# Cosine attention into a two-layer network on one core: one DMA transposition for a batch's x, two for its q, and a later draw of the later batches

## The chip, the cores and the metric

The kernel runs on one core of one Trainium2 chip. The metric is the device time of one execution in microseconds (us). It is the median of several executions, and before the change it is 295.16 us (three executions, 295.12 to 295.33). Batches are counted from zero here: "batch 2" is the third one.

## The reference, cut to what matters

```python
# q, k, v: [B=8, H=8, S=576, D=64] float32;  w_in: [512, 2048];  w_out: [2048, 512]
theta = pi / 2 * arange(S) / S
phi(x) = concat([max(x, 0) * cos(theta), max(x, 0) * sin(theta)], axis=-1)     # 64 -> 128 features
kv  = einsum('bhsf,bhsd->bhfd', phi(k), v)
z   = phi(k).sum(over s)
num = einsum('bhsf,bhfd->bhsd', phi(q), kv)
den = einsum('bhsf,bhf->bhs', phi(q), z) + 1e-6
x   = (num / den), heads side by side       # [B * S = 4608 tokens, 512]
h   = x @ w_in
out = max(0.01 * h, h) @ w_out              # [4608, 512] float32
```

## The kernel before, in words

**Tiling.** The 576 positions of a batch are cut into 512 ("main", four tiles of 128, index `j`) and 64 ("tail"). The main parts of the eight batches are groups `g` = 0 to 7 of 512 tokens; the eight tails together are group 8. A group goes through these stages:

- `load_q`, `load_k`, `load_v`: 1 MB each from HBM (`load_main`, L81), and 64-row tails of k and v in two small transfers each (`load_kvtail`, L91). All are issued by SyncE (SP).
- `q_prep` (L324): VectorE (DVE) writes phi(q) for one `j`, two instructions, into `qp`. `k_tail` and `k_main` (L247, L240) do the same for k into `kpt` and `kpm`; `v_main` and `v_tail` (L252, L255) cast v to 16 bits, on ScalarE (ACT) for batches 3 to 7.
- `q_transpose_dma` (L332): SP issues one DMA transposition for each `j`, `qp` to `qpT`. For batches 0 and 1 TensorE (PE) does it instead (`q_transpose`, L349).
- `kv_all` (L282): 40 small matmuls into a bank pair of PSUM, copied by ACT to `kv`. The ones appended to v make z a further column.
- `num` (L358): 8 matmuls of 66 columns, then `divide` (L372) on DVE, three instructions, which write `xs`. The pool `ps_n` has one buffer, so the `num` of the next `j` waits for the `divide` of this one.
- `x_transpose_dma` (L344) for each `j`: `xs` to `xT` by DMA. Batches 0 and 1 use PE (`x_transpose_half`), and batch 2 has PE transpositions of its own in four steps (`x_transpose`, L425): four 128x128 transpositions and an ACT copy each.
- `ffn1` (L434): for each of 16 tiles `m` of the hidden width, four matmuls of 512 columns of `xT`; ACT applies the leaky ReLU to two `m` at a time from `ps_h` (two buffers) to `g`.
- `ffn2` (L453): `g` times w_out into `ps_o`, four matmuls for each of 16 units, DVE copies each finished tile (`ffn2_out`, `osb`), and SP sends it out.

**Order.** The order is written out by hand, and each engine runs its own instructions strictly in that order. Groups 0 and 1 are a straight list. From there on `units` is the list of TensorE's `ffn1` and `ffn2` units, each at a position: a group takes 16 positions and 32 units, so half a position is one unit of four matmuls. `weave` (L588) puts every other step before the first unit whose position is not smaller. The steps' positions are set by `load_steps`, `kv_steps`, `q_steps` and `out_steps` (L692 to L716). The units of group g begin at position 16 g. They start with the first `ahead` units of `ffn2` of g alone, then `ffn1` of g+1 and the rest of `ffn2` of g alternate, and what is left of `ffn1` of g+1 ends the row.

**Buffers.** `qpp` (4), `qpT` (6), `xs` (4) and `xT` (2) are rotating pools; `qpp` also lends buffers to the x of groups 0 and 1. Each DMA carries one of eight completion semaphores in turn, so in the built program a DMA is issued only when the eighth DMA before it has landed.

Of the kernel before, what the change touches and what calls it, by code (L numbers as in the profile page):

```python
# [9 lines left out]
dt = mybir.dt  # L10
# [3 lines left out]
P = 128  # L14
J = 4
# [3 lines left out]
def kernel(  # L19
# [37 lines left out]
    kvtail = pool("kvtail", 4)  # L57
    qtail = pool("qtail", 2)
    kppool = pool("kpp", 2)
    qppool = pool("qpp", 4)  # L60
    qptpool = pool("qpT", 6)
    xspool = pool("xs", 4)
    small = pool("small", 3)
    xtpool = pool("xT", 2)
    gpool = pool("g", 2)
# [257 lines left out]

    def q_prep(g, j, lo=0, hi=H, eng=DVE):  # L324
        src, c, _ = q_src(g, j)
        if lo == 0:
            st["qp", g, j] = qppool.tile([P, H, F], dt.float16, name="qp", tag="qp")
        qp = st["qp", g, j]
        phi_half(eng, qp[:, lo:hi, 0:D], src[:, lo:hi], cos_t[:, c : c + 1])
        phi_half(eng, qp[:, lo:hi, D:F], src[:, lo:hi], sin_t[:, c : c + 1])  # L330

    def q_transpose_dma(g, j):  # L332
        qpT = qptpool.tile([P, H, P], dt.float16, name="qpT")
        nc.sync.dma_start_transpose(
            out=qpT, in_=st["qp", g, j].rearrange("p h f -> p (h f)")
        )
        st["qpT", g, j] = qpT

    def xT_tile(g, j):
        if ("xT", g) not in st:  # L340
            st["xT", g] = xtpool.tile([P, NKC, MAIN], dt.float16, name="xT")
        return st["xT", g][:, :, j * P : (j + 1) * P]

    def x_transpose_dma(g, j):  # L344
        nc.sync.dma_start_transpose(
            out=xT_tile(g, j), in_=st["xs", g, j].rearrange("p h d -> p (h d)")
        )

    def q_transpose(g, j, eng, where="h"):  # L349
        qp = st["qp", g, j]  # L350
        ps = psum(where, [P, H, P], dt.float16, "ps_qt")
        for h in range(H):
            nc.tensor.transpose(ps[:, h, :], qp[:, h, :], ident)  # L353
        qpT = qptpool.tile([P, H, P], dt.float16, name="qpT")
        copy(eng, qpT, ps)
        st["qpT", g, j] = qpT

    def num(g, j, where="n"):  # L358
        qpT = st["qpT", g, j]
        ps = psum(where, [P, 2, 512], dt.float32, "ps_num")  # L360
        for h in range(H):
            for b, lo, hi in q_src(g, j)[2]:
                nc.tensor.matmul(  # L363
                    ps[lo:hi, h // 4, (h % 4) * NE : (h % 4 + 1) * NE],
                    lhsT=qpT[:, h, lo:hi],
                    rhs=kv[b][:, h, :],
                )
        xs = xspool.tile([P, H, D], dt.float16, name="xs")
        divide(ps, xs.rearrange("p (a b) e -> p a b e", a=2))
        st["xs", g, j] = xs  # L370

    def divide(ps, xs):  # L372
        den = small.tile([P, H], dt.float32, name="den")
# [15 lines left out]

    def num_half(g, jp, hg, where, ps=None):  # L390

        if hg == 0:
            st["xp", g, jp] = qppool.tile([P, 2, H, D], dt.float16, name="xp", tag="qp")
# [10 lines left out]
        divide(ps, st["xp", g, jp][:, :, 4 * hg : 4 * hg + 4, :])  # L404

    def x_transpose_half(g, jp, hg, ps=None):

        if ("xT", g) not in st:
            st["xT", g] = xtpool.tile([P, NKC, MAIN], dt.float16, name="xT")
        xp = st["xp", g, jp]  # L410
        out = ps is None
        if out:
            ps = psum("o", [P, 2, 2 * P], dt.float16, "ps_xth")
        for cc in range(2):
            for o in range(2):
                h = 4 * hg + 2 * cc
                nc.tensor.transpose(  # L417
                    ps[:, cc, o * P : (o + 1) * P], xp[:, o, h : h + 2, :], ident
                )
        if out:  # L420
            nc.scalar.copy(
                st["xT", g][:, 2 * hg : 2 * hg + 2, jp * 2 * P : (jp + 1) * 2 * P], ps
            )

    def x_transpose(g, j, where="o"):  # L425
        xs = st["xs", g, j]
        ps = psum(where, [P, NKC, P], dt.float16, "ps_xt")
        for c in range(NKC):
            nc.tensor.transpose(ps[:, c, :], xs[:, 2 * c : 2 * c + 2, :], ident)
        nc.scalar.copy(xT_tile(g, j), ps)  # L430

    def ffn1(g, m, lo=0, hi=MAIN, chunks=range(NKC), where="h"):  # L434

        if ("g", g) not in st:
            st["g", g] = gpool.tile([P, NFT, MAIN], dt.float16, name="g")
        if m % 2 == 0 and chunks[0] == 0 and lo == 0:
            st["h", m // 2] = psum(where, [P, 2, MAIN], dt.float32, "ps_h")
        xT = st["xT", g]  # L440
        ps = st["h", m // 2]
        for c in chunks:
            nc.tensor.matmul(  # L443
                ps[:, m % 2, lo:hi],
                lhsT=w1[m // 4, c][0][:, w1[m // 4, c][1], m % 4 : 512 : 4],
                rhs=xT[:, c, lo:hi],
                start=(c == 0 and lo == 0),
                stop=(c == NKC - 1 and hi == MAIN),
            )
        if m % 2 == 1 and chunks[-1] == NKC - 1 and hi == MAIN:  # L450
            nc.scalar.activation(st["g", g][:, m - 1 : m + 1, :], ps, AF.Lrelu)  # L451
# [202 lines left out]
    ps = psum("h", [P, 2, MAIN], dt.float16, "ps_x")  # L654
    for jp in range(2):
        x_transpose_half(1, jp, 0, ps[:, :, jp * 2 * P : (jp + 1) * 2 * P])
    nc.vector.tensor_copy(st["xT", 1][:, 0:2, :], ps)
    ffn2_out(0, 0, ACT)
    ffn2_mm(0, 1, 15, 16)
    ffn2_out(0, 1, ACT)  # L660
# [16 lines left out]
    for m in range(6, NFT):  # L677
        units.append((8 + m / 2, f1(1, m)))
    for g in range(1, NG):
        ahead = {1: 8, 2: 4}.get(g, 0)  # L680
        order = [f2(g, i) for i in range(ahead)]
        for i in range(16):
            if g + 1 < NG:
                order.append(f1(g + 1, i))
            if ahead + i < 16:
                order.append(f2(g, ahead + i))
        for n, u in enumerate(order):
            units.append((16 * g + 16 * n / len(order), u))
# [3 lines left out]
    def kv_steps(b, start, step, mm, eng_v, n_act=0):  # L692
        at(start - 0.01, kp_tiles, b)
        at(start, k_tail, b, DVE, DVE)
        for i in range(J):
            at(start + (i + 1) * step, k_main, b, i, ACT if i < n_act else DVE, DVE)
        v0, dv = (start + 1.5 * step, 1) if b > 3 else (start + 3 * step, 0.1)
        at(v0, v_main, b, 0, 4, eng_v)
        at(v0 + dv, v_main, b, 4, 8, eng_v)
        at(v0 + 2 * dv, v_tail, b, eng_v)  # L700
        at(mm, kv_all, b)
# [6 lines left out]
    def out_steps(b, start, step, lag):  # L708
        for j in range(J):
            at(start + j * step, num, b, j)  # L710
            at(start + j * step + lag, x_transpose_dma, b, j)

    def q_steps(b, start, step, lag):
        for j in range(J):
            at(start + j * step, q_prep, b, j)
            at(start + j * step + lag, q_transpose_dma, b, j)  # L716

    q_steps(2, 8, 0.4, 0.3)
    kv_steps(2, 9.7, 0.5, 14, DVE, 2)
# [56 lines left out]
```

## Time and profile before

| What | Value |
|---|---|
| median of three executions | 295.16 us |
| the profiled execution, its own time | 295.4 us |
| its span (first to last instruction) | 293.6 us |
| TensorE busy | 286.6 us, 98% |
| VectorE, ScalarE, GpSimd busy | 128.7, 118.3, 12.6 us |
| granted TensorE clock | 0.999 of full speed |
| DMA packets | 88,933, of which 56,912 under 512 B |
| HBM read and written | 36.70 and 9.44 MB |

The profiled execution is one execution, 0.24 us above the median. About 1.8 us of its time lie outside the span. Matmuls overlap in TensorE's pipeline, so the mean duration of one in the table of groups (373 to 379 ns for 512 columns) is longer than the distance from one start to the next: 0.86 us for four, 216 ns each, in the chain of waits.

### The profile page before, as it was taken

How to read it: one execution, taken by the hardware profiler on the slowest of the kernel's cores; microseconds unless marked ns; L12 is line 12 of the kernel's file. 1: busy time of each engine (PE TensorE's matmuls, PEld its weight loads, DVE VectorE, ACT ScalarE, POOL GpSimd, SP SyncE). 2: the span in 40 equal slices, each digit the busy share in tenths (PEclk: the TensorE clock that was granted, in tenths of full speed). 3: DMA queues.
4: the chain of work that ended last, by engine and by line, in shares of the span. 5: the costliest groups of instructions: out<-in, count | busy, mean ns of one | idle time of the engine just before them, and what ended most of it. 6: DMA issues, size and time to landing. Idle time of an engine off the chain costs nothing.

```text
span 293.6 us, 4865 instructions
## 1 busy us (share of the span) xinstructions
PE 286.6 (98%) x1958; PEld 152.6 (52%) x1958; DVE 128.7 (44%) x328; ACT 118.3 (40%) x148; POOL 12.6 (4%) x24
## 2 busy tenths in 40 slices
PE   8899999999999998999999999999999999999995
PEld 3585466555555554555545554555444444444444
DVE  6841687936836714923562346233333311000011
ACT  6856266753544631642453226322222232222200
POOL 2264000000000000000000000000000000000000
PEclk9999999999999999999999999999999999999999
DMA  7999999999999999989664998716671211011133
GB/s 230 346 387 407 321 362 335 313 193 334 200 285 320 180 258 343 163 173 332 170 148 84 279 259 180 111 54 143 136 169 56 71 54 38 36 45 59 42 70 73
DMA packets 88933, 56.93 MB, mean 194 GB/s; under 512 B 56912, under 2 KB 81744, under 8 KB 88528
## 3 DMA queue, kind: packets, MB, share of 16 engines
q1 hardware_dynamic: 88832, 56.57, 74.3%
q8 instruction: 15, 0.25, 0.4%
q10 hardware_dynamic: 80, 0.07, 0.1%
q14 instruction: 6, 0.05, 0.0%
HBM read 36.70 MB, written 9.44 MB: 157 GB/s over the span
## 4 chain that ended last, share of the span: by engine, by line
PE 88%; DMA 6%; SPq 3%; DVE 1%; ACT 1%; issue 0%; DVEq 0%
PE ps_h L443 40%; PE ps_o L466 39%; DMA ktl<-in_k_dram 3%; PE ps_num L363 2%; PE ps_kv L299 2%; DMA vst<-in_v_dram 2%; SPq L96 1%; SPq L86 1%; DMA out_dram<-osb 1%; PE ps_xth L417 1%; PE ps_qt L353 1%; PE ps_numh L399 1%; PE ps_kv L290 0%; PE ps_idle L166 0%; PE ps_kvh L274 0%
## 5 line engine op out<-in xcount | busy, mean ns | idle before, releaser
L443 PE MATMUL ps_h<-xT,w 128*128 128x512 f16 (+1 forms) x592 | 142.8, 373 | 0.1
L466 PE MATMUL ps_o<-w,g 128*128 128x512 f16 x560 | 139.5, 379 | 0.0
L451 ACT ACTIVATE g<-ps_h 128x1024 f16<-128x1024 f32 x72 | 73.2, 1023 | 125.2 <-PE ps_h L443 125.2
L443 PEld LDWEIGHTS <-w 128*128 128x128 f16 x592 | 64.4, 114 | 52.3 <-issue 0.2
L466 PEld LDWEIGHTS <-g 128*128 128x128 f16 x560 | 54.2, 98 | 61.4
L234 DVE COPY osb<-ps_o 128x512 f32<-128x512 f32 x31 | 21.4, 691 | 79.3 <-PE ps_o L466 78.5
L374 DVE TENSOR_SCALAR den<-ps_num 128x8 f32<-128x8 f32 x28 | 4.6, 165 | 51.0 <-PE ps_num L363 51.0
L379 DVE TENSOR_TENSOR xs<-ps_num,rden 128x512 f16<-128x512 f32 x28 | 19.4, 691 | 1.0
L226 DVE TENSOR_SCALAR kpm<-kst,sin_t 128x512 f16<-128x512 f32 (+1 forms) x40 | 16.6, 430 | 1.3 <-DMA kst<-in_k_dram 1.3
L226 DVE TENSOR_SCALAR qp<-qst,cos_t 128x512 f16<-128x512 f32 (+1 forms) x34 | 15.5, 456 | 2.7 <-DMA qst<-in_q_dram 2.7
L226 DVE TENSOR_SCALAR qp<-qst,sin_t 128x512 f16<-128x512 f32 (+1 forms) x34 | 15.5, 456 | 0.0
L232 ACT CAST vmain<-vst 128x1024 f16<-128x1024 f32 (+1 forms) x14 | 12.8, 919 | 6.0 <-DMA vst<-in_v_dram 5.9
L363 PEld LDWEIGHTS <-qpT 128*128 128x128 f16 (+1 forms) x256 | 10.6, 101 | 8.4 <-issue 3.1
L226 DVE TENSOR_SCALAR kpm<-kst,cos_t 128x512 f16<-128x512 f32 (+1 forms) x29 | 13.2, 454 | 0.4 <-DMA kst<-in_k_dram 0.3
L363 PE MATMUL ps_num<-kv,qpT 128*128 128x66 f16 (+1 forms) x256 | 11.8, 194 | 0.9 <-DVE xs L379 0.9
L166 PE MATMUL ps_idle<-blank 128*128 128x512 f16 x30 | 10.0, 483 | 1.2 <-DVE blank L161 1.2
L234 DVE CAST w<-w2st 128x1024 f16<-128x1024 f32 (+1 forms) x6 | 5.1, 868 | 11.5 <-DMA w2st<-in_moe_w_out_dram 11.4
L232 ACT COPY qpT<-ps_qt 128x1024 f16<-128x1024 f16 x7 | 7.0, 1012 | 6.0 <-PE ps_qt L353 6.0
L234 POOL CAST w<-w1st 128x1024 f16<-128x1024 f32 (+1 forms) x9 | 8.5, 946 | 3.4 <-DMA w1st<-in_moe_w_in_dram 3.3
L378 DVE RECIPROCAL rden<-den 128x8 f32<-128x8 f32 x36 | 7.3, 203 | 1.2
L299 PE MATMUL ps_kv<-vmain,kpm 128*128 128x66 f16 x192 | 7.2, 194 | 0.0
L306 ACT CAST kv<-ps_kv 128x528 f16<-128x528 f32 x6 | 3.6, 599 | 7.5 <-PE ps_kv L299 7.5
(62 smaller groups left out, 102.6 us busy)
## 6 DMA issues: line engine op xcount, KB each, us to landing
out_dram<-osb SPq DMA_DIRECT2D x32, 256.0 KB, 2.9
qst<-in_q_dram SPq DMA_DIRECT2D x7, 1024.0 KB, 6.9
kst<-in_k_dram SPq DMA_DIRECT2D x6, 1024.0 KB, 9.8
vst<-in_v_dram SPq DMA_DIRECT2D x6, 1024.0 KB, 9.0
w1st<-in_moe_w_in_dram SPq DMA_DIRECT2D x7, 512.0 KB, 10.3
w2st<-in_moe_w_out_dram SPq DMA_DIRECT2D x3, 1024.0 KB, 12.9
kst<-in_k_dram SPq DMA_DIRECT2D x4, 512.0 KB, 7.2
vst<-in_v_dram SPq DMA_DIRECT2D x4, 512.0 KB, 8.1
```

The source lines that it names most:

```text
L166: nc.tensor.matmul(ps, lhsT=blank[:, 0:P], rhs=blank)
L226: eng.tensor_scalar(out=o, in0=i, scalar1=0.0, scalar2=col, op0=ALU.max, op1=ALU.mult)
L232: nc.scalar.copy(o, i)
L234: eng.tensor_copy(o, i)
L299: nc.tensor.matmul(ps[:, h % 2, h // 2], lhsT=kpm[:, h, j, :], rhs=vmain[b % 2][:, h, j, :], start=False, stop=(h >= H - 2 and j == J - 1),)
L363: nc.tensor.matmul(ps[lo:hi, h // 4, (h % 4) * NE : (h % 4 + 1) * NE], lhsT=qpT[:, h, lo:hi], rhs=kv[b][:, h, :],)
L374: nc.vector.tensor_scalar_add(den.rearrange("p (a b) -> p a b", a=2), ps[:, :, D : 4 * NE : NE], 1e-6)
L378: nc.vector.reciprocal(rden, den)
L379: nc.vector.tensor_tensor(out=xs, in0=ps[:, :, 0 : 4 * NE].rearrange("p a (b e) -> p a b e", e=NE)[:, :, :, 0:D], in1=rden.rearrange("p (a ...
L443: nc.tensor.matmul(ps[:, m % 2, lo:hi], lhsT=w1[m // 4, c][0][:, w1[m // 4, c][1], m % 4 : 512 : 4], rhs=xT[:, c, lo:hi], start=(c == 0 an ...
L451: nc.scalar.activation(st["g", g][:, m - 1 : m + 1, :], ps, AF.Lrelu)
L466: nc.tensor.matmul(st["ps_o", g, tt], lhsT=st["g", g][:, m, tt * P : (tt + 1) * P], rhs=w2[:, m, :], start=(m == 0), stop=(m == NFT - 1),)
```

## The change

- q: two `j` share one `qp` tile and one `qpT` tile; `q_transpose_dma` transposes a pair (sixteen 128x128 blocks), two DMAs for a batch instead of four.
- x: `xs` is one tile for the whole batch, and `x_transpose_dma` transposes it in one DMA (sixteen blocks) after the last `divide`, instead of four of four blocks. `xT` is laid out as [128, j, chunk, 128], so the moving operand of `ffn1` is four pieces of 128 columns instead of 512 in a row. The pools become `qpp` 2, `qpT` 3, `xs` 1 of the larger tiles.
- Batch 2's x goes by DMA too; `x_transpose` is gone.
- Order: `ahead` is 14 and 8 instead of 8 and 4 for g = 1 and 2. Batch 3's k and v are loaded at 17.95 and 18 instead of 11 and 13, right behind batch 2's x transposition (17.9). The steps of batches 3 and 4 move later by 1 to 5 positions, the loads of batch 5 by 2, and the k and v steps of batches 5 to 7 by 1.5 at a step of 1.2 instead of 1.4.

```diff
-    qppool = pool("qpp", 4)
-    qptpool = pool("qpT", 6)
-    xspool = pool("xs", 4)
+    qppool = pool("qpp", 2)
+    qptpool = pool("qpT", 3)
+    xspool = pool("xs", 1)
...
-    def q_transpose_dma(g, j):
-        qpT = qptpool.tile([P, H, P], dt.float16, name="qpT")
+    def q_transpose_dma(g, jp):
         nc.sync.dma_start_transpose(
-            out=qpT, in_=st["qp", g, j].rearrange("p h f -> p (h f)")
+            out=qpT_pair(g, jp).rearrange("p o h t -> p (o h) t"),
+            in_=st["qp2", g, jp].rearrange("p o h f -> p (o h f)"),
         )
...
-            st["xT", g] = xtpool.tile([P, NKC, MAIN], dt.float16, name="xT")
-        return st["xT", g][:, :, j * P : (j + 1) * P]
+            st["xT", g] = xtpool.tile([P, J, NKC, P], dt.float16, name="xT")
+        return st["xT", g]
...
-    def x_transpose_dma(g, j):
+    def x_transpose_dma(g):
         nc.sync.dma_start_transpose(
-            out=xT_tile(g, j), in_=st["xs", g, j].rearrange("p h d -> p (h d)")
+            out=xT_tile(g).rearrange("p j c t -> p (j c) t"),
+            in_=st["xs", g].rearrange("p j h d -> p (j h d)"),
         )
...
-                rhs=xT[:, c, lo:hi],
+                rhs=xT[:, lo // P : hi // P, c, :],
...
-    nc.vector.tensor_copy(st["xT", 1][:, 0:2, :], ps)
+    nc.vector.tensor_copy(
+        st["xT", 1][:, :, 0:2, :], ps.rearrange("p c (j t) -> p j c t", j=J)
+    )
...
-        ahead = {1: 8, 2: 4}.get(g, 0)
+        ahead = {1: 14, 2: 8}.get(g, 0)
...
-        v0, dv = (start + 1.5 * step, 1) if b > 3 else (start + 3 * step, 0.1)
+        v0, dv = (start + 1.5 * step, 1) if b > 3 else (start + 2 * step, 0.5)
...
-            at(start + j * step + lag, x_transpose_dma, b, j)
+        at(start + (J - 1) * step + lag, x_transpose_dma, b)
...
-            at(start + j * step + lag, q_transpose_dma, b, j)
+            if j % 2:
+                at(start + j * step + lag, q_transpose_dma, b, j // 2)
...
-    for j in range(J):
-        at(14.5 + 1.1 * j, num, 2, j)
-        at(15.8 + 1.1 * j, x_transpose, 2, j, "o" if j < 2 else "h")
-
-    load_steps(3, 11, 13, 10)
-    q_steps(3, 18, 0.8, 0.8)
-    kv_steps(3, 20, 0.7, 24, ACT)
-    out_steps(3, 24.5, 1.4, 1)
-
-    load_steps(4, 21.4, 22.5, 21.3)
-    kv_steps(4, 28, 1.2, 34, ACT)
-    q_steps(4, 30, 0.8, 0.8)
-    out_steps(4, 36.8, 2, 1.6)
+    out_steps(2, 14.4, 0.9, 0.8)
+
+    load_steps(3, 17.95, 18, 10)
+    q_steps(3, 18.5, 0.8, 0.8)
+    kv_steps(3, 24, 0.7, 27.8, ACT)
+    out_steps(3, 28.3, 1, 1)
+
+    load_steps(4, 26, 27.2, 25.9)
+    kv_steps(4, 31, 1.2, 37.5, ACT)
+    q_steps(4, 31.5, 0.8, 0.8)
+    out_steps(4, 38.5, 1.8, 1.6)
...
-            load_steps(b, base - 14.5, base - 13, base - 14.6)
-            kv_steps(b, base - 9.5, 1.4, base - 2, ACT)
+            late = 2 if b == 5 else 0
+            load_steps(b, base - 14.5 + late, base - 13 + late, base - 14.6 + late)
+            kv_steps(b, base - 8, 1.2, base - 2, ACT)
```

More of the change, by code (lines that the diff above doesn't have):

```diff
@@ L325, in q_prep @@
         src, c, _ = q_src(g, j)
-        if lo == 0:
-            st["qp", g, j] = qppool.tile([P, H, F], dt.float16, name="qp", tag="qp")
+        if lo == 0 and j % 2 == 0:
+            st["qp2", g, j // 2] = qppool.tile([P, 2, H, F], dt.float16, name="qp")
+            for o in range(2):
+                st["qp", g, j + o] = st["qp2", g, j // 2][:, o]
         qp = st["qp", g, j]
@@ L330, in q_prep, with qpT_pair, xT_tile @@
         phi_half(eng, qp[:, lo:hi, D:F], src[:, lo:hi], sin_t[:, c : c + 1])
-    def q_transpose_dma(g, j):
-        qpT = qptpool.tile([P, H, P], dt.float16, name="qpT")
+    def qpT_pair(g, jp):
+        t = qptpool.tile([P, 2, H, P], dt.float16, name="qpT")
+        for o in range(2):
+            st["qpT", g, 2 * jp + o] = t[:, o]
+        return t
+    def q_transpose_dma(g, jp):
         nc.sync.dma_start_transpose(
-            out=qpT, in_=st["qp", g, j].rearrange("p h f -> p (h f)")
-        )
-        st["qpT", g, j] = qpT
-    def xT_tile(g, j):
+            out=qpT_pair(g, jp).rearrange("p o h t -> p (o h) t"),
+            in_=st["qp2", g, jp].rearrange("p o h f -> p (o h f)"),
+        )
+    def xT_tile(g):
         if ("xT", g) not in st:
-            st["xT", g] = xtpool.tile([P, NKC, MAIN], dt.float16, name="xT")
-        return st["xT", g][:, :, j * P : (j + 1) * P]
-    def x_transpose_dma(g, j):
+            st["xT", g] = xtpool.tile([P, J, NKC, P], dt.float16, name="xT")
+        return st["xT", g]
+    def x_transpose_dma(g):
         nc.sync.dma_start_transpose(
-            out=xT_tile(g, j), in_=st["xs", g, j].rearrange("p h d -> p (h d)")
+            out=xT_tile(g).rearrange("p j c t -> p (j c) t"),
+            in_=st["xs", g].rearrange("p j h d -> p (j h d)"),
         )
@@ L353, in q_transpose @@
             nc.tensor.transpose(ps[:, h, :], qp[:, h, :], ident)
-        qpT = qptpool.tile([P, H, P], dt.float16, name="qpT")
-        copy(eng, qpT, ps)
-        st["qpT", g, j] = qpT
+        if j % 2 == 0:
+            qpT_pair(g, j // 2)
+        copy(eng, st["qpT", g, j], ps)
     def num(g, j, where="n"):
@@ L367, in num @@
                 )
-        xs = xspool.tile([P, H, D], dt.float16, name="xs")
-        divide(ps, xs.rearrange("p (a b) e -> p a b e", a=2))
-        st["xs", g, j] = xs
+        if j == 0:
+            st["xs", g] = xspool.tile([P, J, H, D], dt.float16, name="xs")
+        divide(ps, st["xs", g][:, j].rearrange("p (a b) e -> p a b e", a=2))
     def divide(ps, xs):
@@ L390, in num_half @@
     def num_half(g, jp, hg, where, ps=None):
-        if hg == 0:
-            st["xp", g, jp] = qppool.tile([P, 2, H, D], dt.float16, name="xp", tag="qp")
+        if hg == 0 and jp == 0:
+            st["xs", g] = xspool.tile([P, J, H, D], dt.float16, name="xs")
         if ps is None:
@@ L403, in num_half @@
                 )
-        divide(ps, st["xp", g, jp][:, :, 4 * hg : 4 * hg + 4, :])
+        divide(ps, st["xs", g][:, 2 * jp : 2 * jp + 2, 4 * hg : 4 * hg + 4, :])
     def x_transpose_half(g, jp, hg, ps=None):
-        if ("xT", g) not in st:
-            st["xT", g] = xtpool.tile([P, NKC, MAIN], dt.float16, name="xT")
-        xp = st["xp", g, jp]
+        xT, xs = xT_tile(g), st["xs", g]
         out = ps is None
@@ L417, in x_transpose_half @@
                 nc.tensor.transpose(
-                    ps[:, cc, o * P : (o + 1) * P], xp[:, o, h : h + 2, :], ident
+                    ps[:, cc, o * P : (o + 1) * P], xs[:, 2 * jp + o, h : h + 2, :], ident
                 )
@@ L421, in x_transpose_half @@
             nc.scalar.copy(
-                st["xT", g][:, 2 * hg : 2 * hg + 2, jp * 2 * P : (jp + 1) * 2 * P], ps
-            )
[L425 to L430, printed above, removed]
+                xT[:, 2 * jp : 2 * jp + 2, 2 * hg : 2 * hg + 2, :],
+                ps.rearrange("p c (o t) -> p o c t", o=2),
+            )
     def ffn1(g, m, lo=0, hi=MAIN, chunks=range(NKC), where="h"):
```

## The prediction

> **What bounds the kernel now.** I read the page's busy times first, then TensorE's groups by shape, then TensorE's waits, then the chain of waits around the longest one.
>
> ```profile
> PE 286.6 (98%) x1958; PEld 152.6 (52%) x1958; DVE 128.7 (44%) x328; ACT 118.3 (40%) x148; POOL 12.6 (4%) x24
> ```
>
> TensorE is the bound. VectorE and ScalarE are under half busy, so work taken from them is worth nothing by itself. Only two things shorten the span: instructions taken out of TensorE's list, and waits taken out of it. TensorE's groups (busy us, mean ns | idle before):
>
> ```profile
> L466 PE MATMUL ps_o<-w,g 128*128 128x512 f16 x560 | 139.5, 379 | 0.0
> L443 PE MATMUL ps_h<-xT,w 128*128 128x512 f16 x560 | 138.7, 379 | 0.1
> L363 PE MATMUL ps_num<-kv,qpT 128*128 128x66 f16 x192 | 10.0, 194 | 0.9 <-DVE xs L379 0.9
> L429 PE MATMUL ps_xt<-ident,xs 128*128 128x128 f16 x16 | 1.5, 218 | 0.0
> ```
>
> The 1120 big matmuls have no idle time to lose, and 216 ns each (four per 0.86 us in the chain) are 242 us that the change keeps. Two entries can go: L429, and the 0.9 us before L363. The sixteen L429 lie in four places like this (timeline, TensorE alone):
>
> ```profile
> 66.38 0.39 PE L429 MATMUL ps_xt<-ident,xs 128*128 128x128 f16 x4
> 66.60 1.89 PE L466 MATMUL ps_o<-w,g 128*128 128x512 f16 x8
> ```
>
> The next unit starts 0.22 us after the first transposition, so four of them take 0.22 us of the list, not the 0.39 that pipelining shows. The chain around the wait of L363:
>
> ```profile
> 105.85 8.51 DMA ktl<-in_k_dram
> ...
> 114.46 0.62 DVE kpt L226 x2
> 115.08 0.09 DVE den L374
> ...
> 115.42 0.70 DVE xs L379
> 116.12 0.14 issue
> 116.26 0.42 PE ps_num L363 x8
> ```
>
> Batch 5's k tail lands at 114.36. VectorE stands at `k_tail` from 110.65 on (3.8 us in the waits), and the `divide` of batch 4's second `num` is queued behind it. The third `num` needs its PSUM buffer, so it starts at 116.26. The unit before it started at 114.33 and lasts 0.86, so TensorE loses 1.07 us. Nearly all other idle time of TensorE lies in the first 20 us and behind the last matmul, where the change has nothing.
>
> **The change, part by part.** *Removed.* Batch 2's transpositions: 4 x 0.22 = 0.90 us, all on the path. Their four ACT copies (0.58 us each) lie beside TensorE: nothing. [...]
>
> *Moving operand in four pieces.* No row shows a moving operand in pieces. Below it cannot cost less than the 216 ns of a contiguous one. Above, the nearest row is the strided weight read of L443 (113 ns against 98 for the contiguous L466), 15% more. I take zero, since pieces of 128 columns are much nearer to contiguous than a read of every fourth element; the far end is 15% of 560 x 0.216 = 18 us, kept as a small chance. [...]
>
> *The transposition of sixteen blocks.* From the tiles' views:
>
> ```profile
> DMA to landing us min/median/max: 3.0/3.3/6.9
> DMA to landing us min/median/max: 2.4/3.7/6.5
> ```
>
> The first is `qpT` (8 blocks), the second `xT` (4 blocks). Twice the blocks add 0.6 us at the minimum, so 16 blocks land in 2.4 + 3 x 0.6 = 4.2 us on a straight line. Proportional to the blocks it would be 4 x 2.4 = 9.6. I take 4.2, because the two rows lie on a line with a large constant. Issue on SP takes 1.22 and 1.26 us at the median, so 1.3 for sixteen; in a full queue three q transpositions land 0.86 us apart, so 1.8 us of transfer for a pair.
>
> *Batch 2.* Up to the first `num` of batch 2 (63.28) TensorE's list is unchanged. From there each unit is 0.864 and each `num` 0.26: the fourth `num` ends at 69.5 and the fourth `ffn2` unit at 70.36. DVE's `divide` (1.33 from the end of `num` to `xs`) is done at 70.85. The `osb` copy and its DMA stand before the x transposition on SP, so that is issued at 72.0 and lands at 76.2. The first `ffn1` of group 2 comes after ten more `ffn2` units (`ahead` is 14), at 79.0. Slack 2.8, cost zero.
>
> *Batch 3's k and v, issued behind that wait.* k goes out at 73.3. A lone 1 MB load lands in 5.8 us (batch 6's q, 129.01 to 134.79), and the next one 3.1 to 3.4 later (batch 6's and batch 4's k). So k lands at 79.1, its tails at 79.5, v at 82.7. DVE needs k at 80.9. ACT's chain is tighter: `ffn1` of group 2 runs without `ffn2` between, so an activation (1.02) is due every 1.73 us, and the two v casts (0.95 each), the tails (0.8) and the `kv` copy (0.6) go into the gaps of 0.7. Stepping through these, `kv` comes late for `num` (89.8) once v lands after 83.3. Slack 0.6: zero, but each later microsecond is paid.
>
> *Batch 4.* TensorE goes on by the same steps: batch 3's `kv_all` (1.3) from 87.65, its `num` at 89.8, 91.8, 93.8 and 95.8, the last `ffn1` of group 2 to 96.9, eight `ffn2` units to 103.8. On the DMA queue, batch 3's v tail ends at 83.2; three `osb` (0.65 each) and two q pairs (1.8 each) follow, to 88.8; q, k and the k tail of batch 4 to 95.6, v and its tail to 99.2. DVE reaches `k_tail` at 95.4 and the `divide` of batch 3's last `num` is due at 96.2, so that ends at 97.6, and the x transposition issued then lands behind v near 101.7. `ffn1` of group 3 wants it at 103.8. Slack 2: zero.
>
> *Batch 5, the old stall.* The load moves 2 positions later, its use 1.5, but `ahead`, fewer DMAs and batch 4's later place move both sides. SP's list has batch 4's q pairs ahead; the second waits for DVE's last q step (102.8) and takes 1.3 to issue, so q goes out at 104.2, lands at 110.0, k at 113.2 to 113.9 (before, k5 took 3.9 us behind q5) and its tail 0.4 later. TensorE has batch 4's `kv_all` at 106.4 and its `num` at 109.4, 113.2 and 116.9. DVE now reaches `k_tail` at 113.1, behind an `osb` copy, and a q step (0.79) stands between it and the `divide`. `k_tail` must start by 114.2: 0.53 for itself, 0.79, 1.13 for the `divide` and 0.14 to TensorE make 116.8. I take the stall as gone but for an expected 0.1: -1.07 + 0.1. Its far end is 1.1, as before. Batch 4's x is issued at 122 and due at 128.2, slack 2.
>
> *Batches 6 to 8.* Loads stay, uses come 1.5 positions (2.6 us) later, x lands more than 7 positions before its `ffn1`. Nothing. SP issues 21 transpositions instead of 52, which frees a queue that was not the bound.
>
> Sum for the profiled execution: 295.4 - 0.90 - 1.07 + 0.1 = 293.5; it stands 0.24 above the median, so 293.3 for the median.
>
> **The rivals.** *A: one of the two tight feeds is late* (v of batch 3, k of batch 5). For: both margins are under 0.6 us, and loads of the same size differ by 0.8 us in the trace (3.07 to 3.93 behind each other). Against: the x transposition is cheaper in the queue than the loads that stood there. One feed late by a microsecond gives 294.3; it eats the gain from 2 us on.
>
> *B, slower: the time of a transposition goes with its blocks.* Then x lands 9.6 us after issue. It decides once landing takes over 7.0 us for batch 2 and 6.1 for batches 3 and 4. Batch 2's `ffn1` waits 81.6 - 79.0 = 2.6; k and v land behind it, v at 88.4 against 85.9, 2.5; batches 3 and 4 wait 3.5 and 3.4. Sum 12.0, so 305.3. For: one DMA in place of four cannot start before the last `divide`, and nothing shows sixteen blocks. Against: eight blocks land hardly later than four. [...]
>
> *C: the pieces of the moving operand cost.* Up to 18 us, 311; against it stands the above.
>
> **How the numbers follow.** Forecast, no new stall worth 0.3 us: 0.60, at 293.3. A: 0.28, from 293.6 to 295.0 and mostly under 294.6. B: 0.08. C and other mishaps: 0.04. The range reaches from 292.9 (no stall at all, another 0.2 for the spread of runs) into A, to 294.9; what is left out is B, C and the end of A. A measurement of this kernel tells about 0.2% from no change, 0.59 us. Faster (under 294.57): 0.60 and two thirds of A, 0.79. The same: 0.09. Slower: 0.12, B and C.
>
> **What the profile after would show.** TensorE's busy time about 0.9 us lower, no L429 group, and no idle before the `num` of batch 4. The x transposition of batch 2 landing 4 to 5 us after issue, before 79. Wrong if: TensorE's group of `ffn1` or of `num` shows an idle time that an x or q transposition or `kv` ended; `xT` lands 7 us or more after issue; `k_tail` of batch 5 still ends in a wait that `num` shows; or four `ffn1` matmuls take more than 0.86 us.

## The result

| | Kernel before | Changed kernel |
|---|---|---|
| median of six executions each | 295.14 us | 305.43 us |
| lowest and highest | 294.59, 295.62 us | 304.00, 306.47 us |
| the profiled execution: its time, its span | 295.4, 293.6 us | 304.98, 303.2 us |
| mean granted TensorE clock | 0.999 | 0.994 |

The changed kernel is slower: the ratio is 1.0343, with a 95% interval from 1.0311 to 1.0376. The forecast was 293.3 us, in a range that ended at 294.9. Rival B's price of 305.3 is within 0.2 us of the measured time by coincidence, for its mechanism did not happen: no transposition of sixteen blocks took 9.6 us.

**The profile after.** First the page's busy times and the row of the clock:

```profile
PE 288.4 (95%) x1942; PEld 152.0 (50%) x1942; DVE 128.3 (42%) x328; ACT 116.1 (38%) x144; POOL 12.7 (4%) x24
...
PEclk9999999999999979999999999999999999999999
```

The sixteen transpositions are gone (1958 - 16 = 1942 matmuls), yet TensorE is busy 1.8 us longer and its share falls from 98% to 95%. One slice in 40 shows a lowered clock. (The other five executions have a mean clock of 0.989. The profiled one has one stretch of 3.4 us at half clock and 0.994, so 0.989 is what two such stretches would make: an estimate from these numbers.) TensorE's groups (busy us, mean ns | idle before, its largest releaser):

```profile
L445 PE MATMUL ps_h<-xT,w 128*128 128x512 f16 (+1 forms) x592 | 143.4, 375 | 5.6 <-DMA xT<-xs 4.3
L468 PE MATMUL ps_o<-w,g 128*128 128x512 f16 x560 | 138.4, 380 | 0.0
L373 PE MATMUL ps_num<-kv,qpT 128*128 128x66 f16 (+1 forms) x256 | 11.8, 194 | 3.2 <-DVE xs L389 3.2
```

`ffn1` had 0.1 us of idle before and has 5.6 now, and `num` has 3.2 in place of 0.9. TensorE's waits name the three places (us in total, times, longest):

```profile
PE ps_h L445 <- DMA xT<-xs: 4.3, 1, 4.3
PE ps_num L373 <- DVE xs L389: 3.2, 1, 3.2
PE ps_h L445 <- ACT g L453: 1.2, 1, 1.2
```

By the matmuls' starts in the trace TensorE has three losses in a row. It loses 1.41 us at 87.21, in `ffn1` of group 2, waiting for an activation that stands behind the cast of batch 3's v. It loses 4.42 us at 109.74, where the first `ffn1` of group 3 waits for batch 3's x, and 3.38 us at 127.75, at batch 4's third `num`, the place of the old stall. The second is followed by 3.4 us at half clock (two windows, 109.5 to 112.9 and the next; the seventh value is the granted clock):

```profile
109.50:112.90 3.40, 3.16 (x8) 1.18 (x9) 2.46 (x6) 0.00 (x0) 0.00 (x0) 0.50 1.06 220
112.90:116.30 3.40, 3.40 (x51) 2.07 (x49) 0.00 (x0) 1.62 (x2) 0.00 (x0) 1.00 0.95 196
```

Of the eight matmuls there, seven are followed by the next one only after 0.41 to 0.43 us instead of 0.216: 1.54 us in all. With smaller waits of 0.18, 0.34 and 0.21 the losses are 11.5 us. Less 1.07 (the old stall stood in the same place) and less the 0.90 of the transpositions, that is 9.5 of the 9.6 us by which the spans differ.

The third loss comes from the same delay as the second. VectorE at `k_tail` of batch 4 (timeline, with the idle time before it), the chain of waits behind it, SP's entries in the same stretch (start, duration), and the end of the chain:

```profile
102.79 0.35 DVE L226 TENSOR_SCALAR kpt<-ktl,cos_t 128x256 f16<-128x256 f32 x1 [5.90 <-DMA ktl<-in_k_dram]
```

```profile
104.36 0.87 DVE qp L226 x2
105.23 0.79 DVE kpm L226 x2
106.02 1.58 DVE qp L226 x4
107.60 0.79 DVE kpm L226 x2
108.39 0.60 DVE osb L234
108.99 0.79 DVE qp L226 x2
```

```profile
106.88 3.39 SPq L342 DMA_TRANSPOSE qpT<-qp  x1
110.36 0.53 SPq L482 DMA_DIRECT2D out_dram<-osb  x1
111.00 2.13 SPq L342 DMA_TRANSPOSE qpT<-qp  x1
113.22 0.85 SPq L86 DMA_DIRECT2D qst<-in_q_dram  x1
```

```profile
116.83 8.23 DMA ktl<-in_k_dram
...
125.43 0.35 DVE kpt L226
125.78 0.79 DVE qp L226 x2
...
126.91 0.69 DVE xs L389
```

Batch 4's k tail lands at 102.69. VectorE stood 5.90 us in front of `k_tail` and then works off what is queued behind it, without a pause, until 112. SP's next entries wait for q steps among this work, the last of which ends at 109.79. SP itself is in the way too: the issue of batch 4's first q pair holds it until 110.27, although the output behind it was ready at 108.99, and that of the second until 113.13. So batch 5's q goes out at 113.22, and its k tail lands at 125.06. `k_tail`, a q step and the `divide` follow, as before, 10.7 us later in the kernel than before.

### The profile page after: what moved, and what is told of

Same layout as the page of the kernel before. It is cut to its first block, busy times and chain, and to the rows that moved or that the text cites. A ratio compares the mean times of both kernels' runs of the same rounds, so it can differ in the third digit from the quotient of the medians.

```text
span 303.2 us, 4739 instructions
## 1 busy us (share of the span) xinstructions
PE 288.4 (95%) x1942; PEld 152.0 (50%) x1942; DVE 128.3 (42%) x328; ACT 116.1 (38%) x144; POOL 12.7 (4%) x24
## 4 chain that ended last, share of the span: by engine, by line
PE 73%; DMA 10%; DVE 7%; SPq 7%; ACT 1%; issue 1%; DVEq 0%; ACTq 0%
PE ps_h L445 34%; PE ps_o L468 32%; DMA ktl<-in_k_dram 5%; DMA vst<-in_v_dram 5%; SPq L96 3%; DVE kpm L226 2%; DVE qp L226 2%; PE ps_num L373 2%; SPq L86 2%; PE ps_kv L299 1%; PE ps_l L497 1%; SPq L342 1%; DVE xs L389 1%; DVE osb L234 1%; SPq L354 1%
## 5 line engine op out<-in xcount | busy, mean ns | idle before, releaser
L373 PEld LDWEIGHTS <-qpT 128*128 128x128 f16 (+1 forms) x256 | 10.6, 101 | 10.9 <-DMA vtl<-in_v_dram 3.7
L166 PE MATMUL ps_idle<-blank 128*128 128x512 f16 x30 | 10.3, 494 | 1.2 <-DVE blank L161 1.2
L226 DVE TENSOR_SCALAR kpt<-ktl,cos_t 128x256 f16<-128x256 f32 x8 | 2.8, 349 | 14.6 <-DMA ktl<-in_k_dram 14.6
## 6 DMA issues: line engine op xcount, KB each, us to landing
w1st<-in_moe_w_in_dram SPq DMA_DIRECT2D x7, 512.0 KB, 10.1
```

Source lines behind the costliest of these rows:

```text
L166: nc.tensor.matmul(ps, lhsT=blank[:, 0:P], rhs=blank)
L226: eng.tensor_scalar(out=o, in0=i, scalar1=0.0, scalar2=col, op0=ALU.max, op1=ALU.mult)
L373: nc.tensor.matmul(ps[lo:hi, h // 4, (h % 4) * NE : (h % 4 + 1) * NE], lhsT=qpT[:, h, lo:hi], rhs=kv[b][:, h, :],)
```

## The experiments

Ratios are to the kernel before on the same chip, with 95% intervals. Landing times and waits are from the trace of each kernel's profiled execution. In the split run of experiment 1 and in the runs of experiments 2 and 5 that execution was the longest of the four (303.91, 306.27 and 306.69 us): its trace tells which waits there are, and not what makes the median.

**1. Blocks or order?** Four kernels. The changed order with each sixteen-block transposition as two of eight, one after the other:

```diff
-        nc.sync.dma_start_transpose(
-            out=xT_tile(g).rearrange("p j c t -> p (j c) t"),
...
+        for jp in range(2):
+            nc.sync.dma_start_transpose(
+                out=xT_tile(g)[:, 2 * jp : 2 * jp + 2].rearrange("p j c t -> p (j c) t"),
...
```

> Changed kernel, every step in its place, but each transposition DMA of sixteen blocks goes out as two of eight, back to back. Theory Q (queue): a transposition of sixteen blocks holds SyncE's list until the DMAs ahead of it have landed (3 to 4 us in place of 1.2), and that made batch 4's and 5's loads late. It expects SyncE's median for one transposition at 1.2 to 1.4 us, batch 4's q issued by 87 instead of 90.9, and a time of 295 to 300 us. Theory O (order): the places of the loads alone make them late, whatever the size of a transposition. It expects 304 to 307 us.

Measured: 301.79 us, ratio 1.0197 (1.0111 to 1.0283). Batch 4's q is issued at 90.69, as in the changed kernel (90.92), and its k lands at 100.54. By the medians a third of the loss goes (3.6 us; the interval allows 2 to 7) and two thirds stay: between the ranges of the two theories. An issue holds SP for 1.3 us at the median, as theory Q said, but there are twice as many, and the step by which the theory would have it, an earlier issue of batch 4's q, does not show.

The other way round, the order of before (batch 2's x by TensorE, the old positions) with one transposition for x and two for q:

```diff
-            at(start + j * step + lag, x_transpose_dma, b, j)
+        at(start + (J - 1) * step + lag, x_transpose_dma, b)
...
-            at(start + j * step + lag, q_transpose_dma, b, j)
+            if j % 2:
+                at(start + j * step + lag, q_transpose_dma, b, j // 2)
```

> Kernel before with its own order, batch 2's x by TensorE as before, but q in transpositions of sixteen blocks (a pair) and x of the other batches in one of sixteen after the last divide. Theory Q: SyncE is held here too, loads of batches 4 and 5 go out 2 to 4 us late and the old stall of 1.07 us before batch 4's third num grows; 297 to 301 us. Theory O: the size of a transposition costs nothing, 294.8 to 295.6 us, with the stall of about 1.07 us as before.

Measured: 294.09 us, ratio 0.9966 (0.9938 to 0.9994), and no `num` among TensorE's waits. In the order of before the merging does no harm, against theory Q; the old stall is gone, and batch 5's k tail lands at 112.11 instead of 114.36. This kernel also has the moving operand in four pieces and the permuted copy, so neither of these costs anything that shows. Its median is the lowest of the study, below both kernels.

The changed kernel with batch 3's k and v drawn as early as before:

```diff
-    load_steps(3, 17.95, 18, 10)
+    load_steps(3, 11, 13, 10)
```

> Changed kernel, but batch 3's k and v are loaded at positions 11 and 13, as before, not behind batch 2's x transposition. Theory O: batch 4's loads go out about 5 us earlier, the waits at batch 3's v, batch 3's x and batch 5's k tail go: 293 to 296 us. Theory Q: only the first wait (1.4 us, batch 3's v) goes for certain; transpositions still hold SyncE ahead of batch 4's and 5's loads: 297 to 304 us.

Measured: 299.06 us, ratio 1.0123 (1.0049 to 1.0198): 6.4 of the 10.3 us come back from one line. (The interval of this run is wide; it allows 4 to 9.) Batch 3's x lands at 102.61 instead of 109.69 and nothing waits for it. What is left (TensorE's waits):

```profile
PE ps_num L373 <- DVE xs L389: 2.7, 1, 2.7
...
PE ps_h L445 <- DMA xT<-xs: 1.0, 1, 1.0
```

The first is batch 5's `k_tail` again, with 3.4 us at half clock behind it. The second is new: x of batch 2, now behind both loads on SP, lands at 79.54.

And the kernel before with batches 5 to 7 drawn as in the changed one:

```diff
-            load_steps(b, base - 14.5, base - 13, base - 14.6)
-            kv_steps(b, base - 9.5, 1.4, base - 2, ACT)
+            late = 2 if b == 5 else 0
+            load_steps(b, base - 14.5 + late, base - 13 + late, base - 14.6 + late)
+            kv_steps(b, base - 8, 1.2, base - 2, ACT)
```

> Kernel before with one part of the change alone: batch 5's loads two positions later and the k and v steps of batches 5 to 7 as in the changed kernel. Both theories take it as harmless by itself: the wait of 1.07 us before batch 4's third num goes, or shrinks below 0.5: 294.0 to 294.7 us. If the later draw of batch 5 is itself at fault, the wait grows to 2 to 3.5 us as in the changed kernel: 296 to 298 us.

Measured: 294.47 us, ratio 0.9965 (0.9930 to 1.0001); the stall at the third `num` is gone. So each of these two parts alone does no harm, and both remove the stall; what they gain, 0.7 to 1.1 us, is about what the forecast gave for it, though the second interval just includes no gain. What is left to make the loss is the order around batches 2 to 4, in which the merging costs its third as well. The larger `ahead` and the later draw of batch 4 were not tried by themselves.

**2. In front of the loads, or just late?** The changed order, but batch 2's x by TensorE, so that only an output stands ahead of batch 3's k and v:

```diff
...
-    out_steps(2, 14.4, 0.9, 0.8)
+    for j in range(J):
+        at(14.4 + 0.9 * j, num, 2, j)
+        at(15.4 + 0.9 * j, x_transpose, 2, j, "o" if j < 2 else "h")
```

> The changed order with every late draw kept (batch 3's k and v at 17.95 and 18), but batch 2's x transposed by TensorE as before, so that nothing stands ahead of the two loads on SP but output. Theory T (the x transposition in front of the loads is what makes them late): batch 3's k lands about 3 us earlier, near 78.5 instead of 81.4, its v near 82 instead of 85.1; the 1.4 us wait of ffn1 goes, x of batch 3 is issued 2 to 3 us earlier, and the 4.4 us wait before group 3 shrinks below 2 and keeps the clock: 305.4 + 0.9 (transpositions on TensorE) - 1.4 - 2.5 - 1.6 = 300.8, range 299 to 302. Theory D (drawn too late, whatever stands ahead): all waits stay within 1 us, 304.5 to 306.5.

Measured: 302.98 us, ratio 1.0275 (1.0197 to 1.0354). Theory T's named step fails. k from issue to landing, in the changed kernel and in this one:

```profile
DMA to landing us min/median/max: 7.4/7.4/7.4
DMA to landing us min/median/max: 8.3/8.3/8.3
```

v lands at 85.09 and 85.06. Without the transposition ahead of them the loads come no earlier: drawn at this place they are there at 85 with it or without it. The first wait fell away for another reason: TensorE itself came 1.9 us later to this stretch, 0.9 of it by the transpositions and 1.0 by waits earlier in the execution. Batch 3's x came 1.1 us earlier and its wait was 3.08; batch 4's third `num` waited 5.42, with 6.8 us at half clock around it. What brings the median between the two theories' ranges is not shown, since this is the trace of the longest execution.

**3. Does the idle time lower the clock?** Fourteen matmuls that compute nothing, where `ffn1` of group 3 waits:

```diff
+    at(35.9, idle, 14)
```

> The changed kernel with 14 matmuls that compute nothing put on TensorE right before the first ffn1 of group 3, where it waits 4.42 us and then runs 3.4 us at half clock (8 matmuls, 0.43 us apart). Their output is not read. Theory I (the idle time itself lowers the clock, and the matmuls at half rate are a price of 1.6 us on top of the wait): the wait for x stays, the remaining idle is about 1.4 us, the clock stays at 1.0, and the time falls to 303.8. Theory N (the drop of the clock has another cause, or is only a matter of records): the same time as the changed kernel, 305.4, or more by what the matmuls take beyond the wait.

Measured: 304.21 us, ratio 1.0293 (1.0240 to 1.0347). That is 1.2 us less than the changed kernel, but the intervals overlap. The same two windows as above show a clock of 1.00 and 1.00:

```profile
109.50:112.90 3.40, 3.14 (x15) 1.49 (x15) 3.18 (x8) 0.00 (x0) 0.00 (x0) 1.00 1.08 228
112.90:116.30 3.40, 3.40 (x40) 1.86 (x38) 0.00 (x0) 0.67 (x1) 0.00 (x0) 1.00 1.03 189
```

The blanks themselves waited 2.9 us for a PSUM buffer, so the idle stretch was shortened, not closed; in this execution that was enough. (Two of the other three have a mean clock of 0.992 and 0.994, so some half clock somewhere.) This is what theory I says of the clock: the half clock comes with the idle time (4.26 us of it and then a clock of 0.50 in the changed kernel, 2.91 us and 1.00 here). That the time falls by it is not shown. Batch 3's x landed at 109.87, and the fourteen matmuls, which started only at 109.76, kept TensorE until 112.78; the profiled span is 303.0 us, against 303.2.

**4. What makes a load lag?** Batch 4's k lands 4.62 us behind its q in the changed kernel, batch 5's 4.86; the prediction had 3.1 to 3.4, and 3.2 to 3.9 for batch 5. In each of these stretches the trace has a packet of a queue of its own (the DMA queues between 113.0 and 124.4 in the changed kernel):

```profile
q1 hardware_dynamic: 4907, 3.47, 103.7%
q8 instruction: 1, 0.02, 0.6%
```

The profile gives the queue's kind as `instruction`; that the packet is a piece of program code for TensorE is borne out below, where matmuls added to the list move it. The profile of the changed kernel counts fifteen on this queue, 0.25 MB, so 16 KB each; one occupies a DMA engine for about 1.05 us (0.88 to 1.45), and between two there are 93 to 154 matmuls, 123 in the mean. That a load then waits for one engine is the author's reading of the end of batch 5's v (windows of the changed kernel; the eighth value is the DMA share, the last GB/s):

```profile
126.00:127.00 1.00, 0.00 (x0) 0.00 (x0) 0.93 (x5) 0.00 (x0) 0.00 (x0) 1.00 0.85 263
127.00:128.00 1.00, 0.25 (x8) 0.28 (x9) 1.00 (x3) 0.00 (x0) 0.00 (x0) 1.00 0.08 30
128.00:128.50 0.50, 0.50 (x9) 0.26 (x6) 0.50 (x2) 0.00 (x0) 0.00 (x0) 1.00 0.08 18
```

For 1.5 us the share of the 16 engines is 0.08, about one sixteenth, as when fifteen are done and one is not, and v lands only at 128.54. To move the pieces, the 30 blank matmuls of the first 16 us became 8 of the same width and 83 thin ones, 61 more, in the changed kernel and in the one before:

```diff
-        for _ in range(n):
+        wide, thin = {14: (8, 23), 7: (0, 26), 6: (0, 22), 1: (0, 4)}[n]
+        for _ in range(wide):
             nc.tensor.matmul(ps, lhsT=blank[:, 0:P], rhs=blank)
+        for _ in range(thin):
+            nc.tensor.matmul(ps[:, 0:32], lhsT=blank[:, 0:P], rhs=blank[:, 0:32])
```

> The changed kernel with 61 more matmuls in TensorE's list in the first 16 us: of the blank ones that fill its waits there, 21 of 512 columns and 35 of... in short, 14 + 7 + 6 + 3 blanks become 8 wide and 83 of 32 columns, in about the same time. Nothing else is moved. TensorE's code is fetched in pieces of 16 KB, one for about 123 matmuls, and a piece occupies one DMA engine for about 1.05 us; with 61 more matmuls each piece is fetched 8 to 11 us earlier: 78.5 to about 69, 99.1 to about 90.5, 121.7 to about 111. Theory F (a piece of code on one of the 16 DMA engines holds that engine's share of a load, and the load lands with its last share): batch 4's k lands 3.1 to 3.5 us behind its q instead of 4.6, batch 5's 3.1 to 3.5 behind instead of 4.9, batch 3's k in about 6.5 us instead of 7.45; the three waits of 1.41, 4.42 and 3.38 us lose about 1 us each or more, so 305.4 becomes 300 to 302.5. Theory R (loads lag for another reason and the pieces of code only happen to fall there): the lags stay at 4.6 and 4.9, and the time within 1 us of 305.4.

Measured in the changed kernel: 302.67 us, ratio 1.0258 (1.0220 to 1.0296), 2.8 us less, and 0.2 above the end of theory F's range. The pieces moved to 68.5, 91.4 and 110.3, and batch 4's and 5's k land 3.34 and 3.07 us behind q. Batch 5's k from issue to landing, in the changed kernel and in this one:

```profile
DMA to landing us min/median/max: 10.3/10.3/10.3
DMA to landing us min/median/max: 8.5/8.5/8.5
```

For batch 4 the same figure went only from 10.6 to 10.1: its piece now fell behind the issue of q, and q landed 0.7 us later. The three waits are 0.95, 3.54 and 1.93 us: all shorter, none gone. Over all profiles of this study, k landed 3.07 to 3.78 us behind q in the forty cases without a large piece of code from 3 us ahead of q's landing to k's, and 3.20 to 5.42 in the twenty-four with one; the medians are 3.33 and 3.83.

> The same 61 matmuls in the kernel before. Its piece of code at 110.5, inside batch 5's q and k loads, moves to about 101.5, in front of them. Theory F: k of batch 5 lands 3.1 to 3.5 us behind q instead of 3.93, so the wait of 1.07 us before batch 4's third num shrinks to about 0.5: 295.15 - 0.6 = 294.5. Theory R: no change, 295.0 to 295.4, or slower by what the thin matmuls take at the start.

Measured in the kernel before: 295.74 us, ratio 1.0016 (0.9989 to 1.0044), a miss for theory F's time. Its lag did shrink, from 3.93 to 3.14, but the piece now fell at 103.5, ahead of batch 5's q, which landed at 111.31 instead of 110.03; the stall stayed at 1.06. This profile also has two stretches of 3.4 us at half clock in the first 18 us, and its mean clock is 0.988. Five of the twelve executions have 0.987 or 0.988 and one 0.994, and none of the 23 of the kernel before on that chip is under 0.998, so here the half clock comes with the thin matmuls (the changed kernel with them has a stretch there as well). The six executions at 0.998 or more took 294.39 to 295.42 us, about the time of the kernel before. For theory F's 294.5 this run is inconclusive.

**5. Do outputs and transpositions take turns on SP?** In the changed kernel SP issues like this behind batch 3's loads (start, duration):

```profile
81.15 0.52 SPq L482 DMA_DIRECT2D out_dram<-osb  x1
81.78 4.22 SPq L342 DMA_TRANSPOSE qpT<-qp  x1
86.50 0.36 SPq L482 DMA_DIRECT2D out_dram<-osb  x1
86.97 3.22 SPq L342 DMA_TRANSPOSE qpT<-qp  x1
90.30 0.53 SPq L482 DMA_DIRECT2D out_dram<-osb  x1
90.92 0.39 SPq L86 DMA_DIRECT2D qst<-in_q_dram  x1
```

The issue of a pair holds SP for 4.22 and 3.22 us, until 86.00 and 90.19. The outputs ahead of them land at 86.08 and 90.09. The outputs of groups 1 to 4 were given to GpSimd's queue:

```diff
-            nc.sync.dma_start(rows[:, tt, :], osb)
+            (nc.gpsimd if 0 < g < 5 else nc.sync).dma_start(rows[:, tt, :], osb)
```

> The changed kernel with the output tiles of groups 1 to 4 sent out by GpSimd's queue instead of SP's, so that no output stands between two transpositions or between a transposition and a load on SP. In the changed kernel batch 3's two q pairs land at 88.06 and 92.31, each behind an output that had to land first, and batch 4's q is issued at 90.92. Theory S (the sixteen-block transpositions and the outputs take turns on SP, each turn at the full latency of an output): the pairs land 2 to 2.6 us apart, batch 4's q goes out near 88 and its k lands near 99, x of batch 3 comes 2 to 3 us earlier, and the 4.4 us wait shrinks to 2 or less, without half clock; 305.4 becomes 300 to 302. Theory V (the pairs wait for batch 3's v, and what follows waits for the sum of bytes, in whatever order): batch 4's q goes out within 1 us of 90.9 and the time is within 1 us of 305.4.

Measured: 305.03 us, ratio 1.0315 (1.0272 to 1.0358), no gain that this can tell. Theory S has the direction of each local step: the pairs land 1.26 us apart instead of 4.25, batch 4's q goes out at 89.54 (the theory said near 88; the first pair itself landed 1.4 us later), its k lands at 99.14, and batch 3's x at 106.35, 3.3 us earlier. The wait for it is gone. And the time stays, as TensorE's waits show:

```profile
PE ps_num L373 <- DVE xs L389: 6.8, 1, 6.8
PE ps_h L445 <- ACT g L453: 2.1, 1, 2.1
```

TensorE comes to batch 4's third `num` earlier and waits there for batch 5's k tail (123.80, against 125.06), 6.97 us in place of 3.38, and 6.8 us at half clock begin within the wait. The losses stand in a row, and the last of them sets the end.

**6. A version that keeps the merging and the DMA for batch 2's x?** First batch 3 early and batch 5's k and v steps behind batch 4's last `num`:

```diff
-            kv_steps(b, base - 8, 1.2, base - 2, ACT)
+            if b == 5:
+                kv_steps(5, 43.95, 0.6, 47.2, ACT)
+            else:
+                kv_steps(b, base - 8, 1.2, base - 2, ACT)
```

> Batch 3's k and v loaded early as in the run before it (299.06), and batch 5's k and v steps moved behind the last num of batch 4. Theory Q1 (a k_tail of batch 5 that waits for its late tail stands ahead of batch 4's divide on VectorE, and that is all that is left): the wait of 2.86 us before batch 4's third num and the 3.4 us at half clock behind it (1.65) go, so 299.06 - 4.5 = 294.5, clock back to 0.998 or more. Theory L (batch 5's k and v are simply too late for TensorE, wherever their steps stand): the wait moves to batch 5's kv_all or to its num, 2 us or more of it, and the time stays at 297 to 299.

Measured: 296.98 us, ratio 1.0066 (1.0029 to 1.0103). The wait before the third `num` and its half clock are gone; the median is 2.1 us below that of experiment 1's run with batch 3 early, though the intervals overlap. In the profiled execution two others stand instead: 3.03 us for batch 2's x, which lands at 81.47 behind batch 3's loads, and 1.5 us of `kv_all` for the cast of batch 5's v tail. Theory Q1 named its step rightly and was wrong that it was all; theory L's wait for batch 5's `kv_all` is there too, shorter than the 2 us it named. Then with batches 4 and 5 early as well:

```diff
-    load_steps(4, 26, 27.2, 25.9)
+    load_steps(4, 21.4, 22.5, 21.3)
...
-            late = 2 if b == 5 else 0
+            late = 0
```

> The changed kernel (sixteen-block transpositions, batch 2's x by DMA, later steps) with the loads of batches 3, 4 and 5 back at their earlier positions and batch 5's k and v steps behind batch 4's last num. Theory Q1 (the merged transpositions and the saved TensorE work are worth what was forecast, and only the late loads cost): no wait over 0.3 us in the middle of the span, clock 0.998 or more, 295.15 - 0.9 - 1.0 = 293.2 to 293.9. Theory M (the merged transpositions themselves collide with loads wherever these stand): a wait of 1 us or more for xT, ktl or g remains, 295 or above.

Measured: 296.63 us, ratio 1.0050 (1.0012 to 1.0087), above theory Q1's 293.2 to 293.9. Theory M's time fits, but the profile has no wait of 1 us for the tiles that it names; it has `kv_all`'s 1.5 us, and 3.4 us at half clock in the first 18 us. And with `kv_all` at 48 instead of 47.2:

> The run with all loads early (296.63) once more, with batch 5's kv_all at 48 instead of 47.2, so that ScalarE has 1.4 us more for the cast of v's tail that kv_all waited 1.5 us for. If that wait is all that is left in the middle, it goes and the time is 296.63 - 1.4 = 295.2, near the kernel before; a version below both kernels would need 294. If x of batch 2, transposed behind batch 4's loads, is the tight one, a wait for xT shows before group 2 in some executions and the time stays at 296 to 297.

Measured: 296.32 us, ratio 1.0020 (0.9994 to 1.0045), from 294.66 to 299.94. The wait of `kv_all` shrank from 1.5 to 0.63 us. The profiled execution, at 299.24 one of the longer ones and so no measure of the median, again has the wait for batch 2's x of the runs with only batch 3 early:

```profile
PE ps_h L445 <- DMA xT<-xs: 3.0, 1, 3.0
```

x of batch 2 lands at 82.25, and 3.4 us at half clock follow. So with batch 3's loads ahead of it, x of batch 2 comes late (waits of 1.14, 3.03 and 3.15 us in three of the four profiles of this kind); with the loads behind it, they do. No version tried here has the 0.90 us of TensorE's transpositions for nothing.

## Why the prediction was wrong

**What held.** Sixteen blocks land in 4.2 us at the least, and in little more where the queue is free: 4.47 for batch 2's x (issued 71.74, forecast 72.0; landed 76.21, forecast 76.2), and over the kernel (`xT`, then `qpT`):

```profile
DMA to landing us min/median/max: 4.4/4.6/6.1
DMA to landing us min/median/max: 4.2/5.1/7.6
```

That rules out rival B's mechanism. Rival C's too: four `ffn1` matmuls still take 0.86 us at full clock, and the permuted copy at L659 0.69, as at L657 before, and the kernel of experiment 1 that has both in the order of before lost nothing. The 0.90 us are off TensorE's list. The slacks held as well: v of batch 3 was allowed to land at 83.3 and landed 1.8 late, which cost 1.41 + 0.18. Moved on by these and later losses, x was wanted at 105.3 (forecast 103.8), and `k_tail` of batch 5 had to start by 121.9 (114.2 + 1.6 + 4.4 + 1.7); its tail landed 3.2 later, and 3.38 was lost. It is rival A's kind of failure, a tight feed late, but A gave it 1.7 us over the forecast at most, and the time is 12.1 over it.

**What failed: the landing times on the queue.**
- *Batch 3's k and v.* k was issued 0.7 us later than forecast, because the issue of the x transposition held SP for 2.19 us and not 1.3, and took 7.44 us where the sum took 5.8 from batch 6's q. v then came 3.7 behind, as forecast, so both are 2.3 to 2.4 late. In experiment 2 they landed no earlier without the transposition. Without the piece of code k took 6.72 (experiment 4), but v still landed at 85.10. What makes the pair of loads so long here stays open.
- *Outputs and q pairs.* Three outputs and two pairs were put at 5.6 us, each at its own transfer time. They took 9.4 (85.41 to 94.82). A full queue of q transpositions, where that figure came from, has no outputs in between; here each turn costs most of an output's latency (3.59 us for the one issued at 86.50), +3.8. Experiment 5 shows the turns: with the outputs on another queue the pairs are 1.26 us apart. The 1.3 us that the sum gave to an issue of sixteen blocks also failed: a q pair held SP for 2.98 us at the median.
- *Batch 4's q, k and k tail.* 6.8 us forecast, 7.9 measured, +1.1. The piece of code is not all of it: in the split run of experiment 1 no piece falls into this stretch, and it took 7.5.
- Together 2.2 (v's tail) + 3.8 + 1.1 = 7.1, and the k tail lands at 102.69 where 95.6 was said. Batch 3's x, issued behind `k_tail` and the `divide`, lands at 109.69, not 101.7. The slack of 2.1 against a slip of 8.0 is the largest loss.
- *Half clock.* The sum had no price for what an idle TensorE does to its clock: 1.54 us in the profiled execution.
- *Batch 5.* Its k was taken to depend on SP's list and on DVE's last q step at 102.8. That step is itself behind `k_tail` of batch 4 on VectorE and ended at 109.79, so 7.0 us of the slip were handed on; the issues of the two pairs add 2.0. q was issued at 113.22, not 104.2.

The step that fails is thus "Slack 0.6: zero", and with it "Slack 2: zero" and "I take the stall as gone": these three places were put at nothing, the last at 0.1, on landing times that came 2.4, 8.0 and 11 us late, and they cost 1.41, 4.42 and 3.38. The prediction found the tight place and its price per microsecond, and then took every landing at the fast end of the rows: 5.8 us for a load behind transpositions, where the trace of before also has 6.3 and 8.0 (q of batches 5 and 3). Batch 6's q, the row taken for a lone load, was not even quite alone: a q transposition ahead of it landed 1.95 us after its issue. And A was priced as one late feed, though batch 3's v, batch 4's k and batch 5's k hang on each other through SP's and VectorE's lists.

## What to carry to other kernels

Where one queue carries loads, transpositions and outputs, price a step that is moved back by the landing time of everything behind it, from rows with the same neighbours, and follow a slip through each in-order engine to the next load that it releases; a slip is handed on and grows. When taking away one wait leaves the time unchanged, look for the next wait in the row, and start from the earliest cause: one line of early loads gave back 6.4 us, another queue for the outputs 0.4, which is within the noise. Merging transfers was worth about a microsecond (0.2 to 1.8) where the order left their neighbours alone.

## What the runs showed of the hardware

- *A 16 KB piece of code on one DMA engine can delay a whole load.* The piece takes about 1.05 us. With it moved, batch 5's k took 8.5 us from issue to landing instead of 10.3 (experiment 4). Over all profiles, with one in its way k landed 3.83 us behind q at the median and 5.42 at most, without one 3.33 and 3.78. Matmuls far ahead in the list move it, at times only to the load in front: that is where batch 4's piece went in experiment 4.
- *A transposition of sixteen blocks holds SP* until about the landing of the DMA ahead of it: 17 of the 21 issues in the changed kernel ended between 0.59 us before that landing and 0.57 us behind it, the other four 1.05 to 4.12 us behind. Issue took 1.36 to 4.90 us for q pairs, against 1.23 at the least for eight blocks before. What in the queue holds it was not tried.
- *Idle time and the clock.* Behind the first 20 us, idle stretches of TensorE of 1.97, 2.70, 2.98, 3.37, 3.52 and 4.26 us were followed by 3.4 us at half clock, and 6.8 us of it began within those of 5.26 and 6.81; stretches of 1.96, 2.07, 2.87, 2.91 and 3.21 were not. So between 2 and 3.2 us the length alone does not decide. What else does is not shown. The stretches at half clock lasted 3.41 or 6.83 us, and four of the eight idle stretches that led to them were shorter than 3.41.
